# A fused attention and feed-forward kernel: another order of the output copies, another engine for the late ReLUs, and a rearranged end

## The chip, the cores and the metric

The kernel runs on one core of a Trainium2 chip. The metric is device time in microseconds (us) of one execution; lower is better. A core has TensorE (PE in the profile; its weight loads are the row PEld), VectorE (DVE), ScalarE (ACT), GpSimd (POOL) and SyncE (SP). The last one computes nothing and issues DMAs here. Every engine works through its own instructions in order and waits on semaphores for the others.

## The reference

Attention over 8 batches of 8 heads, 576 tokens and 64 columns a head, in which each row keeps only its 32 largest scores, and then a feed-forward layer:

```python
scores = scale * np.matmul(q, k.transpose(0, 1, 3, 2))
kth = np.partition(scores, -32, axis=-1)[..., -32:-31]
scores = np.where(scores >= kth, scores, -1e9)
attn = softmax(scores)                       # over the last axis
x = (attn @ v), heads side by side           # 4608 tokens x 512
h = x @ w_in                                 # 4608 x 2048
g = np.maximum(h, 0.0) + alpha * np.minimum(h, 0.0)
out = g @ w_out                              # 4608 x 512, float32
```

The kernel uses g = (1 - alpha) relu(h) + alpha h. It folds (1 - alpha) into `w_out`, and takes alpha h through a product `w_lin` of the two weight matrices, made once near the start. The output needs ReLU(h) alone, then, plus one small matmul from x.

## The kernel before, in words

All work is in `fast_path` (line 60). `Ordered` (line 17) wraps each engine, so that an engine's instructions run in the order in which the Python code issues them; every instruction's profile line is therefore L32, and groups are told apart by tile names. Only waits between engines are left to the framework. So what follows the code's order is each engine's queue; where two engines meet is a semaphore.

The unit of attention work is a **duo** (line 65): 128 query rows of each of two heads, against 576 keys. There are ND = 144 duos; a pair of heads makes several duos, and four pairs make a batch. The main loop (line 729) has one **slot** n for each duo, and in slot n each engine does a stage of another duo:

- PE: scores of duo n+1 (`st_qk`, tile `ps_sc`, three banks of PSUM with one buffer), weighted values of an older duo (`st_av`, tile `xo`), then feed-forward matmuls: `h_pe` makes one unit of h (16 or 8 matmuls into `ph`), `o_pe` a quarter of one output tile of 128 rows (five matmuls into `pz`). `keep_warm` fills gaps with matmuls on the tile `idle`, which holds zeros.
- ACT: two Sign passes that count entries above a trial threshold (`st_count`, tile `sg`), Exp of a masked duo into `w` (`st_exp`, line 400), at times the copy of a finished output tile from PSUM (`o_act`, line 579, tile `o_sb`), two ReLU passes that make the mask (`st_relu`, tile `r`), and the copy of the next scores out of PSUM (`st_exit`, tile `s_sb`).
- DVE: twelve MAX8 passes over the new scores, the threshold from them (`threshold_steps`; its last step, `turn`, writes `p`, which the Signs of the next slot need), the exact choice (`pick_steps`, tile `KZ`), the division by the softmax sum (`norm_a`, `norm_b`, tile `x`), and ReLU of h (`h_relu`, line 565, tile `gT`).
- POOL: two products a duo that feed the exact choice (`y`), and two subtractions that apply the mask (`s_sb<-s_sb,r`).
- SP: loads, the DMA transposes of `w` into `wT` (`st_wT`, line 405; its pool `three` has three buffers, line 101) and of `x` into `xT` (`st_xT`, line 468), and the stores of outputs.

Around the change: in a slot ACT's order is Signs, Exp, output copy, ReLUs, score copy (lines 745 to 764). Some even slots are **late** (line 743): too many units of h stand in line, so `dve_slot` has PE make one more (line 357) and its ReLU is taken by DVE at once, but from slot 118 on by ACT at the end of the slot (line 780). `h_relu` works from a queue, so the code's order decides which unit a call takes.

After the loop comes the **drain** (lines 815 to 903), written out by hand: the last duos (D = 143) pass their stages; D - 2, D - 1 and D are masked on DVE (`st_mask`: two products `w<-s_sb,KZ,e_sb` each) and D - 3 by Exp as in the loop; all are transposed by SP's DMA, multiplied by v (`st_av`), divided (`normed`, which also issues the DMA transpose into `xT` when a batch row block is complete), and then through h and the output. In the drain the scores' three banks are reused as one tile `spare` (line 818): bank 0 for every second output tile, banks 1 and 2 for the `xo` of the last four duos. Between these stages stand feed-forward calls as filling. The last block of 128 tokens can start its h only when the last duo has been divided and transposed; its 64 matmuls into `ph` and 20 into the output tile end the work, followed by one copy and one store. At the very end all engines read a flag that tells whether a slow general path must run (it doesn't here).

Of the kernel before, what the change touches and what calls it, by code (L numbers as in the profile page):

```python
# [8 lines left out]
FP32 = mybir.dt.float32  # L9
BF16 = mybir.dt.bfloat16  # L10
# [49 lines left out]
def fast_path(tc, q, k, v, moe_w_in, moe_w_out, moe_alpha, out, flag):  # L60
# [32 lines left out]
    with ExitStack() as ctx:  # L93
# [7 lines left out]
        three = pool("three", 3)  # L101
        gp = pool("gp", 4)
        xp = pool("xp", 4)
        ps_s = pool("ps_s", 1, space=PSUM)
        ps_d = pool("ps_d", 1, space=PSUM)
        ps_x = pool("ps_x", 1, space=PSUM)
        ps_h = pool("ps_h", 2, space=PSUM)
        ps_z = pool("ps_z", 1, space=PSUM)

        qv = q.rearrange("b h s d -> (b h) s d")  # L110
        kv = k.rearrange("b h s d -> (b h) s d")
# [204 lines left out]
        def dve_slot(n, f_late):  # L316

            norm = norm_of(n)
            rows = duos_at("count", n)
            picks = [f for m in duos_at("pick", n) for f in pick_steps(m)]  # L320
            s = T["s", n]
            if n % 2 == 0:
                T["up", n // 2] = two.tile([128, 4, NG // 2, 8], FP32, name="up", tag="up")
            up = T["up", n // 2]
            for i in range(2):
                r = 2 * (n % 2) + i
                for g in range(NG):
                    o = 24 * r + 8 * (g // 2)
                    m = DVE.max(out=(lo if g % 2 else up)[:, r, g // 2, :],
                                in_=s[:, i, GW * g:GW * g + GW])  # L330
                    if g % 2:
                        sm(m, [], [(o, o + 8)])
                        if picks:
                            picks.pop(0)()
            turn = None
            if n % 2:
                fold, negate, least, turn = threshold_steps(n // 2)
                fold()
                if n < ND - 1:
                    h_relu()  # L340
                negate()
            else:
                h_relu()
            for d in rows:
                row(d, 0)
            if turn:
                least()
                turn()
            if norm:
                norm_a(norm)  # L350
            for d in rows:
                row(d, 1)
            if norm:
                norm_b(norm)
            if f_late:
                h_pe()
                if n < 118:
                    h_relu()

        stage = {}  # L360

# [23 lines left out]
        def st_y(n):  # L385
            y = two.tile([128, 2, S], FP32, name="y", tag="y")
            sg = T.pop(("sg", n))
            for i in range(2):
                POOL.tensor_tensor(y[:, i, :], T["s", n][:, i, :], sg[:, i, :], ALU.mult)
            T["y", n] = y  # L390
# [20 lines left out]
        def st_av(n):  # L411
            d = duos[n]
            wt = T.pop(("wt", n))
            if ("xo", n // 2) not in T:
                if n < ND - 4:
                    T["xo", n // 2] = ps_x.tile([128, 2, 2, 65], FP32, name="xo", tag="x")
                else:
                    c = 512 * (1 + n // 2 - ND // 2 + 2)
                    T["xo", n // 2] = T["spare"][:, c:c + 260].rearrange("p (a b c) -> p a b c", a=2, b=2)
            xo = T["xo", n // 2][:, n % 2, :, :]  # L420
            for i in range(2):
                if d[0] == "n":
                    p = d[1]
                    for c in range(5):
                        K = 128 if c < 4 else 64
                        PE.matmul(xo[:, i, :], wt[0:K, 5 * i + c, :], v1[p][0:K, c, i, :],
                                  start=(c == 0), stop=(c == 4))
                else:
                    p = d[1 + i]
                    for h in range(2):  # L430
                        for c in range(5):
                            K = 128 if c < 4 else 64
                            PE.matmul(xo[64 * i:64 * i + 64, h, :], wt[0:K, 5 * i + c, 64 * h:64 * h + 64],
                                      v1[p][0:K, c, h, :], start=(c == 0), stop=(c == 4))
# [60 lines left out]
        def mlp_ready(xt, rows):  # L495
            ntok = sum(r[1] for r in rows)
            e_n = 512 // ntok
            tails = len(rows) > 1
            ch = {"done": 0}
            pieces = []  # L500
            for r0, m in rows:
                for o in range(0, m, 128):
                    pieces.append((r0 + o, min(128, m - o)))

            def unit(i):
                if i == 0:
                    ch["g"] = gp.tile([128, NFT, ntok], BF16, name="gT", tag="gT")
                ph = ps_h.tile([128, e_n, ntok], FP32, name="ph", tag="h")
                for e in range(e_n):
                    f = e_n * i + e  # L510
                    for kk in range(4):
                        if tails:
                            PE.matmul(ph[:, e, :].rearrange("p (b q) -> p b q", b=2),
                                      w_in_b[kk][:, 128 * f:128 * f + 128], xt[:, :, kk, :],
                                      start=(kk == 0), stop=(kk == 3))
                        else:
                            PE.matmul(ph[:, e, :], w_in_b[kk][:, 128 * f:128 * f + 128], xt[:, kk, :],
                                      start=(kk == 0), stop=(kk == 3))
                act.append((ch, e_n * i, e_n, ph))
            for i in range(NFT // e_n):  # L520
                soon.append((now[0] + (3 if now[0] < 116 else 2 if now[0] < ND else 0), lambda i=i: unit(i)))

            def part(t0, a):
                gt = ch["g"]
                if a == 0:
                    turns[0] += now[0] >= ND
                    if turns[0] % 2:
                        ch["z"] = T["spare"][:, 0:DMODEL]
                    else:
                        ch["z"] = ps_z.tile([128, DMODEL], FP32, name="pz", tag="z")  # L530
                z = ch["z"]
                if tails:
                    for b in range(2):
                        PE.matmul(z[64 * b:64 * b + 64, :], xt[:, b, a, :], w_lin_b[a], start=(a == 0), stop=False)
                else:
                    PE.matmul(z, xt[:, a, t0:t0 + 128], w_lin_b[a], start=(a == 0), stop=False)
                for f in range(4 * a, 4 * a + 4):
                    PE.matmul(z, gt[:, f, t0:t0 + 128], w_out_b[f // 4][:, f % 4, :],
                              start=False, stop=(f == NFT - 1))
                if a == 3:  # L540
                    stores.append((z, t0, pieces, now[0] + (now[0] < ND)))
            for t0 in range(0, ntok, 128):
                for a in range(4):
                    oq.append((ch, 4 * a + 4, lambda t0=t0, a=a: part(t0, a)))
# [34 lines left out]
        def o_act():  # L579

            if stores and stores[0][3] <= now[0]:
                z, t0, pieces, _ = stores.pop(0)
                o = io.tile([128, DMODEL], FP32, name="o_sb", tag="io")
                ACT.copy(o, z)
                at, left = 0, []
                for r0, m in pieces:
                    if t0 <= at < t0 + 128:
                        left.append((r0, at - t0, m))
                    at += m
                outs.append((o, left))  # L590
# [134 lines left out]
        for n in range(ND):  # L725
# [19 lines left out]
            for m in duos_at("count", n):  # L745
                st_count(m)
                st_y(m)
            for m in duos_at("exp", n):
                st_exp(m)
            if not norm_of(n):  # L750
                run(n, "ld")
            run(n, "lin_out")
            if ready() > 4 or not wide_copy:
                o_act()
            did = o_pe()
            run(n, "w")

# [18 lines left out]
                sm(DVE.tensor_copy(alpha_ps, aps), [], [(304, 320)])  # L776
                ACT.activation(alpha1m, aps, AF.Copy, scale=-1.0, bias=1.0)
            run(n, "scale")
            if late and n >= 118:
                h_relu(ACT)  # L780
            if norm_of(n):
                st_xT(norm_of(n) - 1)
                st_xT(norm_of(n))
# [10 lines left out]
        def st_mask(d):  # L794
# [5 lines left out]
            for i in range(2):  # L800
                DVE.scalar_tensor_tensor(out=w[:, i, 0:S], in0=s_[:, i, :], scalar=kt[:, i:i + 1],
                                         in1=e[:, i, :], op0=ALU.is_ge, op1=ALU.mult)
            st_wT(d)

        def normed(d):
            norm_a(d)
# [7 lines left out]
                    keep_warm()  # L814

        D = ND - 1
        now[0] = ND
        T["spare"] = ps_s.tile([128, 1536], FP32, name="spare", tag="s")
        o_sp()
        st_av(D - 6)  # L820
        h_pe(2)
# [46 lines left out]
        for _ in range(2):  # L868
            h_pe(2)
            h_relu(ACT)  # L870
        st_av(D - 2)
        h_pe(2)
        h_relu(ACT)
        st_av(D - 3)
        normed(D - 2)
        st_av(D - 1)
        h_pe(2)
        h_relu(ACT)
        st_av(D)
        normed(D)  # L880
        now[0] += 2
        o_pe()
# [301 lines left out]
```

## Time and profile before

| what | us |
|---|---|
| median of 3 runs (815.65 to 817.17) | 816.7 |
| the profiled execution's own time | 816.19 |
| its span, first to last instruction | 814.4 |
| PE, DVE, ACT, POOL busy | 734.9, 750.8, 770.4, 748.1 |
| mean granted clock of TensorE (1 is full) | 0.988 |

The profile comes from one execution. Its span leaves 1.79 us of the execution's time outside. A row of a timeline gives start, duration, engine, line, operation, the tiles written and read, shapes and count; a bracket at its end is the idle time before it and what ended it. A row of the chain of waits gives start, duration and the work that the end of the program waited for. A row of a table by stretches gives, for each engine, busy time and in brackets instructions, then the granted clock and the DMA engines' share.

### The profile page before, as it was taken

Reading aid. Unit: us, or ns where it says so; the run is one execution under the profiler, and the core shown is the slowest. Engines: PE = TensorE matmul, PEld = TensorE weight load, DVE = VectorE, ACT = ScalarE, POOL = GpSimd, SP = SyncE. Lnnn points to the kernel's source line nnn. Section 1 sums busy time; section 2 is a strip of 40 time slices with the busy share of each in tenths; the row PEclk is TensorE's granted clock in tenths of the full one; section 3 lists DMA queues with packets and bytes.
Section 4 is the critical chain, followed back from the end, with each engine's and each line's share of the span. In section 5 each row is a group of like instructions: output and inputs, shape, how many; then the busy total and the mean of one; then the engine's idle time right before and its main releaser. Section 6 shows DMA issues by size and latency. Waiting matters only on the chain.

```text
span 814.4 us, 17835 instructions
## 1 busy us (share of the span) xinstructions
PE 734.9 (90%) x5362; PEld 423.5 (52%) x5434; DVE 750.8 (92%) x3459; ACT 770.4 (95%) x1270; POOL 748.1 (92%) x704
## 2 busy tenths in 40 slices
PE   8888899989889998989889998998989999899986
PEld 5334455555545554555545554555545555455663
DVE  4999999999999999999999999999999998999841
ACT  5999999999999999999999999999999999999951
POOL 2999999999999999999999999999999998999930
PEclk9999999999999999999999999999999999999989
DMA  7699996556656565566656565555665664544461
GB/s 158 174 191 185 161 165 115 102 122 125 136 112 132 111 129 118 116 119 134 128 114 128 111 126 122 127 120 107 142 123 122 114 119 100 93 96 75 98 114 37
DMA packets 343497, 100.25 MB, mean 123 GB/s; under 512 B 337424, under 2 KB 337440, under 8 KB 343392
## 3 DMA queue, kind: packets, MB, share of 16 engines
q1 hardware_dynamic: 340240, 91.63, 57.1%
q0 software_dynamic: 1952, 7.09, 3.6%
q8 instruction: 45, 0.74, 0.4%
q14 instruction: 60, 0.49, 0.2%
q10 hardware_dynamic: 1200, 0.30, 0.2%
HBM read 36.71 MB, written 9.44 MB: 57 GB/s over the span
## 4 chain that ended last, share of the span: by engine, by line
DVE 29%; ACT 28%; PE 20%; POOL 10%; issue 8%; DMA 3%; SPq 0%; ACTq 0%; POOLq 0%; DVEq 0%
DVE small L32 9%; ACT r L32 8%; ACT sg L32 7%; DVE p L32 7%; ACT s_sb L32 6%; DVE up L32 6%; PE pz L32 5%; POOL s_sb L32 5%; PE ps_sc L32 5%; ACT w L32 4%; POOL y L32 4%; PE ph L32 4%; DVE gT L32 3%; PE xo L32 2%; DMA wT<-w 2%
## 5 line engine op out<-in xcount | busy, mean ns | idle before, releaser
L32 POOL TENSOR_TENSOR y<-s_sb,sg 128x576 f32<-128x576 f32 x288 | 362.1, 1278 | 23.4 <-ACT sg L32 23.3
L32 POOL TENSOR_TENSOR s_sb<-s_sb,r 128x576 f32<-128x576 f32 x282 | 355.1, 1280 | 9.1 <-ACT r L32 8.7
L32 DVE MAX8 up<-s_sb 128x8 f32<-128x96 f32 x864 | 212.1, 245 | 15.3 <-ACT s_sb L32 15.0
L32 ACT ACTIVATE sg<-s_sb,p 128x576 bf16<-128x576 f32 x288 | 221.4, 774 | 2.8 <-DVE p L32 1.4
L32 DVE MAX8 p<-y 128x8 f32<-128x576 f32 x288 | 215.3, 748 | 7.9 <-POOL y L32 7.3
L32 DVE MAX8 small<-s_sb 128x8 f32<-128x96 f32 x864 | 216.2, 250 | 0.0
L32 ACT ACTIVATE r<-s_sb,KZ 128x576 bf16<-128x576 f32 x282 | 202.6, 769 | 0.3 <-DVE KZ L32 0.3
L32 PE MATMUL ps_sc<-qkT 64*128 64x512 f32 (+2 forms) x768 | 185.0, 572 | 14.7 <-ACT s_sb L32 14.6
L32 ACT ACTIVATE w<-s_sb 128x1152 bf16<-128x1152 f32 x141 | 163.1, 1157 | 1.7 <-POOL s_sb L32 0.9
L32 ACT COPY s_sb<-ps_sc 128x1152 f32<-128x1152 f32 x144 | 159.1, 1105 | 4.1 <-PE ps_sc L32 4.0
L32 PE MATMUL ph<-xT,w_in_b 128*128 128x256 bf16 (+1 forms) x1472 | 150.3, 250 | 5.6 <-ACT qkT L32 3.7
L32 PEld LDWEIGHTS <-w_in_b 128*128 128x128 bf16 x1472 | 120.4, 98 | 47.3 <-issue 10.1
L32 PE MATMUL pz<-w_out_b,gT 128*128 128x512 bf16 x515 | 134.2, 379 | 9.7 <-issue 6.2
L32 PE MATMUL xo<-v,wT 128*128 128x65 bf16 (+1 forms) x1560 | 123.5, 198 | 0.6 <-DMA wT<-w 0.4
L32 PEld LDWEIGHTS <-wT 128*128 128x128 bf16 (+3 forms) x1600 | 98.0, 100 | 33.2 <-DMA wT<-w 3.9
L32 PEld LDWEIGHTS <-gT 128*128 128x128 bf16 x576 | 54.5, 98 | 74.0 <-issue 18.7
L32 PEld LDWEIGHTS ps_sc<-kd,qkT 128*128 128x128 f32 x256 | 38.5, 189 | 98.4 <-issue 98.4
L32 DVE TENSOR_SCALAR gT<-ph 128x512 bf16<-128x512 f32 x126 | 84.8, 673 | 4.8 <-PE ph L32 4.8
L32 PEld LDWEIGHTS ps_sc<-qkT 64*128 64x128 f32 (+1 forms) x768 | 55.7, 170 | 57.9 <-issue 29.2
L32 PE MATMUL ps_sc<-kd,qkT 128*128 128x128 f32 x256 | 63.1, 329 | 0.0
L32 PE MATMUL rest<-idle 128*128 128x512 bf16 x196 | 50.0, 380 | 6.8 <-DVE gT L32 4.7
L32 ACT ACTIVATION_READ_ACCUMULATOR sg<-s_sb,p 128x1 f32 x288 | 56.1, 195 | 0.0
(68 smaller groups left out, 584.2 us busy)
## 6 DMA issues: line engine op xcount, KB each, us to landing
k_st<-in_k_dram SPq DMA_DIRECT2D x64, 128.0 KB, 2.9
v_st<-in_v_dram SPq DMA_DIRECT2D x64, 128.0 KB, 2.8
q_st<-in_q_dram SPq DMA_DIRECT2D x62, 128.0 KB, 2.7
out_dram<-o_sb SPq DMA_DIRECT2D x30, 256.0 KB, 2.5
w_st<-in_moe_w_out_dram POOLq DMA_DIRECT2D x4, 1024.0 KB, 6.5
wT<-w SPq DMA_TRANSPOSE x144, 3.5
w_in_b<-in_moe_w_in_dram POOLq DMA_DIRECT2D x4, 512.0 KB, 6.0
k_st<-in_k_dram SPq DMA_DIRECT2D x32, 32.0 KB, 3.0
```

Source lines behind the costliest of these rows:

```text
L32: ins = self.tc.keep_in_program_order(f(*a, **kw))
```

## The change

It has five parts.

1. In the main loop `o_act()` is called before `st_exp` in place of after it.
2. In late slots from 118 on, ReLU of the extra unit is DVE's, as in earlier slots.
3. In the drain the pool of the scores is closed, and a new pool takes its three banks as three tiles: two `xo2`, one `pz2`. There is no `spare`.
4. The last duo's weights are not transposed by DMA. `turn_w` has PE transpose them in ten steps against an identity, into two PSUM tiles in the banks of `xo` and `pz`; `turned` copies one of these by DVE, one by ACT into a `wT` tile. POOL writes the identity into `idle` at the start of the drain. With it `st_av(D)` moves ahead of `st_av(D - 3)`, and one unit of h moves between `turn_w` and `turned`.
5. The last output tile is copied in halves, columns 256 to 511 by DVE and 0 to 255 by ACT, and stored in halves by SP's and ACT's queues.

```diff
-        ps_s = pool("ps_s", 1, space=PSUM)
...
+        scores = ctx.enter_context(ExitStack())
+        ps_s = scores.enter_context(tc.tile_pool(name="ps_s", bufs=1, space=PSUM))
...
                 h_pe()
-                if n < 118:
-                    h_relu()
+                h_relu()
...
-                    c = 512 * (1 + n // 2 - ND // 2 + 2)
-                    T["xo", n // 2] = T["spare"][:, c:c + 260].rearrange("p (a b c) -> p a b c", a=2, b=2)
+                    T["xo", n // 2] = ps_e.tile([128, 2, 2, 65], FP32, name="xo2", tag=f"x{n // 2 % 2}")
...
-                        ch["z"] = T["spare"][:, 0:DMODEL]
+                        ch["z"] = ps_e.tile([128, DMODEL], FP32, name="pz2", tag="z2")
...
                 o = io.tile([128, DMODEL], FP32, name="o_sb", tag="io")
+                if now[0] > ND and not (soon or hq or act or oq or stores):
+                    DVE.tensor_copy(o[:, 256:512], z[:, 256:512])
+                    ACT.copy(o[:, 0:256], z[:, 0:256])
+                    r0 = pieces[0][0]
+                    ACT.dma_start(out[r0:r0 + 128, 0:256], o[:, 0:256])
+                    SP.dma_start(out[r0:r0 + 128, 256:512], o[:, 256:512])
+                    return
                 ACT.copy(o, z)
...
+            if ready() > 4 or not wide_copy:
+                o_act()
             for m in duos_at("exp", n):
                 st_exp(m)
...
-            if ready() > 4 or not wide_copy:
-                o_act()
             did = o_pe()
...
-            if late and n >= 118:
-                h_relu(ACT)
...
-            st_wT(d)
+            if d < D:
+                st_wT(d)
+
+        def turn_w(d):
+            ps = [p.tile([128, 5, 128], BF16, name="wTp", tag=t) for p, t in ((ps_x, "x"), (ps_z, "z"))]
+            for i in range(2):
+                for c in range(5):
+                    PE.transpose(ps[i][:, c, :], ws[d % 4][:, i, 128 * c:128 * c + 128], idle)
+            return ps
+
+        def turned(d, ps):
+            wt = T["wt", d] = three.tile([128, 10, 128], BF16, name="wT", tag="wT")
+            DVE.tensor_copy(wt[:, 0:5, :], ps[0])
+            ACT.copy(wt[:, 5:10, :], ps[1])
...
         D = ND - 1
+        POOL.tensor_copy(idle, ident_f)
         now[0] = ND
-        T["spare"] = ps_s.tile([128, 1536], FP32, name="spare", tag="s")
+        scores.close()
+        ps_e = pool("ps_e", 1, space=PSUM)
...
         for _ in range(2):
             h_pe(2)
             h_relu(ACT)
+        ps = turn_w(D)
+        h_pe(2)
+        turned(D, ps)
+        h_relu(ACT)
         st_av(D - 2)
+        st_av(D)
         h_pe(2)
         h_relu(ACT)
         st_av(D - 3)
         normed(D - 2)
         st_av(D - 1)
-        h_pe(2)
-        h_relu(ACT)
-        st_av(D)
         normed(D)
```

## The prediction

> **What bounds the kernel now.** I read the page first, then a table by stretches, the waits of each engine in the loop, and the chain of waits and the timelines of the end. The table gives, for each stretch, busy time of PE, PEld, DVE, ACT and POOL, the granted clock, and the DMA share:
>
> ```profile
> 120.00:620.00 500.00, 455.20 (x3297) 263.40 (x3345) 491.83 (x2289) 496.73 (x811) 493.78 (x448) 1.00 0.59 121
> 620.00:770.00 150.00, 141.69 (x1162) 85.32 (x1176) 140.57 (x656) 146.94 (x244) 141.98 (x125) 1.00 0.53 103
> 770.00:814.40 44.40, 32.74 (x320) 22.13 (x324) 15.19 (x33) 17.36 (x30) 11.19 (x12) 0.89 0.36 75
> ```
>
> From 120 to 620 three engines are at 98 to 99%: ACT can't gain from another order of its own instructions, only from less work, and only as far as DVE and POOL follow. From 620 to 770 ACT stays at 98% and DVE falls to 94%. In the last 44.4 us nothing is full: a chain decides there. Its pieces (start, duration, work):
>
> ```profile
> 782.25 5.73 DMA wT<-w
> ...
> 788.02 1.08 PE spare L32 x10
> ...
> 789.20 0.19 DVE KZ L32
> ...
> 789.41 0.43 DVE x L32
> ...
> 789.89 1.04 PE spare L32 x10
> 790.93 1.82 PE ph L32 x16
> 792.75 0.89 PE spare L32 x10
> ...
> 793.97 3.28 PE pz L32 x14
> 797.25 1.79 PE ph L32 x32
> ...
> 806.94 0.59 ACT o_sb L32
> ```
>
> A DMA transpose, that of duo D-3, ends at 787.98. Then come the matmuls of D-3, the division of its pair on DVE, the matmuls of D-1, a unit of h, and the matmuls of D. Only then can the last row block be divided, transposed and sent through h. These timeline rows carry the terms below:
>
> ```profile
> 780.59 3.11 DVE L32 SCALAR_TENSOR_TENSOR w<-s_sb,KZ,e_sb 128x576 bf16<-128x576 f32 x4
> ...
> 782.00 1.96 PE L32 MATMUL ph<-xT,w_in_b 128*128 128x128 bf16 x32
> ...
> 785.77 0.79 PE L32 MATMUL spare<-v,wT 128*128 128x65 bf16 x10 [1.81 <-DMA wT<-w]
> ...
> 786.59 1.93 SPq L32 DMA_TRANSPOSE wT<-w  x1
> ...
> 789.89 1.04 PE L32 MATMUL spare<-v,wT 128*128 128x65 bf16 x10 [0.80 <-DVE x L32]
> ...
> 794.34 1.19 SPq L32 DMA_TRANSPOSE xT<-x  x1
> ...
> DMA to landing us min/median/max: 2.4/2.9/3.4
> ```
>
> The last one is the landing of the two transposes into `xT`; the later one, in a quiet queue, is taken at 2.4.
>
> **The end, step by step.** I redo the chain on the old clock.
>
> *Start.* POOL's write of `idle` is a cast of 128x128; the nearest rows are 0.29 and 0.40 us (below). It stands ahead of the four `y` products in a queue without idle time, so 0 to 0.3 us reach DVE's choice. DVE next waits for PE anyway, so I take 0.1. Two units of h then run from 782.1 to 784.05, and the masked weights of D are ready at 783.7 (780.59 + 3.11).
>
> *Transposes on PE.* Ten weight loads with matmuls of 128 columns; 32 of that size take 1.96 us, 0.061 each, so 0.6 us, to 784.7. They lie in PE's idle time ahead of 785.77. The unit of h moved behind them (16 x 0.061) ends at 785.65, again in that idle time.
>
> *The new wait.* `st_av(D - 2)` runs at 785.8 to 786.65, as its DMA allows. `turned` needs a `wT` buffer, and of three the free one is that of D-2. The trace shows that wait already: SP issued the fourth transpose at 786.59, when `st_av(D - 2)` ended (785.77 + 0.79 = 786.56). So both copies start at about 786.7. Behind ACT's stands one ReLU, and PE's `st_av(D)` waits for both. Their lengths come from rows of the same engines:
>
> ```profile
> L32 DVE COPY qkT<-tps 128x512 f32<-128x512 f32 x31 | 21.0, 678 | 4.8 <-PE tps L32 4.8
> L32 DVE COPY qkT<-tps 128x128 f32<-128x128 f32 x26 | 7.3, 280 | 0.4 <-PE tps L32 0.4
> L32 ACT COPY s_sb<-ps_sc 128x1152 f32<-128x1152 f32 x144 | 159.1, 1105 | 4.1 <-PE ps_sc L32 4.0
> L32 ACT COPY o_sb<-pz 128x512 f32<-128x512 f32 x34 | 19.3, 569 | 6.8 <-PE pz L32 6.8
> L32 ACT COPY qkT<-tps 128x128 f32<-128x128 f32 x6 | 1.6, 271 | 0.0
> L32 POOL CAST v<-v_st 128x256 bf16<-128x256 f32 x64 | 25.3, 399 | 0.0
> L32 POOL CAST v<-v_st 64x128 bf16<-64x128 f32 x32 | 9.3, 289 | 0.0
> ```
>
> DVE's 640 elements extend the first two rows to 0.8 us (0.68 if 16-bit input were quicker), ACT's lie between 569 and 1105 ns, about 0.7. `st_av(D)` then goes from 787.55 to 788.35.
>
> *Rest.* The fourth unit of h ends at 789.3. `st_av(D - 3)`, whose weights are there since 787.98, ends at 790.1. `st_av(D - 1)` writes a bank of its own; the 0.80 us wait for DVE's `x` shows that inside one tile it had to wait although it wrote other columns. It ends at 790.9. Division (0.19 + 0.43 and two handovers) gives the `xT` transpose at 791.6 in place of 794.34, landing at 794.0. Meanwhile PE does three quarters of the output tile before. They took 3.6 us (from 793.64 to 797.25) with a slow start, and I take 3.4: to 794.3. So what is late next is PE again, with the DMA 0.3 us ahead of it. From there the order is the old one. **Gain 2.9 us**, from 794.3 against 797.25.
>
> **The clock.** Part of this hangs on TensorE's clock:
>
> ```profile
> 783.90:787.30 3.40, 1.58 (x26) 1.35 (x26) 0.00 (x0) 0.60 (x1) 0.00 (x0) 1.00 1.17 191
> 787.30:790.70 3.40, 2.24 (x25) 1.44 (x22) 0.61 (x2) 0.60 (x1) 0.00 (x0) 0.50 0.88 162
> ...
> 548.40:551.80 3.40, 2.11 (x15) 1.35 (x16) 3.40 (x11) 3.40 (x7) 3.40 (x4) 1.00 0.51 96
> 551.80:555.20 3.40, 2.85 (x22) 1.62 (x21) 3.37 (x20) 3.40 (x6) 3.40 (x4) 1.00 0.22 46
> ```
>
> After a stretch with PE busy 46% of the time (1.58 of 3.40, one gap of 1.81 us) the clock was 0.50, and the h unit at 790.93 took 1.82 us where the row at 782.00 gives 0.98. After one with 62% (2.11 of 3.40) it stayed 1.00. In the new order the only gaps there are 0.15 and 0.9 us, 70% busy, so I take full speed throughout. The Trainium skill (TensorE: Matmul & The Clock Gate, section Why this matters for your kernels) warns of idle gaps above about 3 us; the gap here was 1.81 us, and the clock fell all the same, so the trace differs. By that page's rule the clock could not fall in the new order and the sum would stand; by the rows a little more idle time would do it, a rival below.
>
> **The last output.** One copy of 569 to 590 ns becomes two of 256 columns, each about halfway between 271 and 569 on ACT, 280 and 678 on DVE: 0.4. Side by side the end comes 0.2 us sooner, one after the other 0.25 us later; halved stores may land somewhat sooner or, on a second queue, not. I take +0.1, between -0.3 and +0.3. The Trainium skill (PSUM — Partial Sum Buffer, section PSUM bank collisions raise a hardware error) says that reads of one bank by ScalarE and VectorE at once collide and have to be kept apart; no row of before shows such a pair. By it the copies would stand in series, and the term would be +0.25.
>
> **The loop.** Rows from the waits of PE (120 to 770 us), of ACT and DVE (629 to 766 or 769; total, times, longest), the late ReLUs on ACT, DVE's ReLU, and one late slot:
>
> ```profile
> PE pz L32 <- ACT o_sb L32: 15.0, 17, 1.5
> ...
> ACT gT L32 <- PE ph L32: 2.3, 3, 0.9
> L32 ACT ACTIVATE gT<-ph 128x512 bf16<-128x512 f32 x7 | 4.2, 599 | 2.4 <-PE ph L32 2.3
> DVE up L32 <- ACT s_sb L32: 6.4, 11, 0.8
> L32 DVE TENSOR_SCALAR gT<-ph 128x512 bf16<-128x512 f32 x126 | 84.8, 673 | 4.8 <-PE ph L32 4.8
> ...
> 645.60 0.26 DVE L32 MAX8 up<-s_sb 128x8 f32<-128x96 f32 x1
> 646.49 0.60 ACT L32 ACTIVATE gT<-ph 128x512 bf16<-128x512 f32 x1 [0.92 <-PE ph L32]
> 650.41 0.17 DVE L32 TENSOR_SCALAR p<-small 128x4 f32<-128x4 f32 x1
> 651.88 0.78 ACT L32 ACTIVATE sg<-s_sb,p 128x576 bf16<-128x576 f32 x1
> ```
>
> *Output copies earlier.* The same instructions on ACT: Exp starts 0.57 us later 30-odd times, and its transpose is used two slots (10 us) later. By its due time in the code (line 541) the tile copied was finished in an earlier slot. PE gets its bank about 1.1 us sooner (Exp's length), which removes most of 15.0 us of PE's waits. But ACT's score copies wait for PE only 4.0 us in the whole execution (their row above), so PE's time is hidden nearly everywhere. I take -0.1, between -4.0 (all those waits gone) and +1.0 (a copy here and there that now waits for PE).
>
> *Late ReLUs.* ACT loses seven (4.2 us) and their waits (2.3): 6.5 us. DVE gains seven of 0.67, 4.7 us, and it must wait for PE's unit too, since it comes to it earlier. In the slot shown DVE would start the ReLU at 646.49 and its next MAX8 at 647.1, not at 645.60: 1.5 late. Its threshold `p` comes at 652.1, not at 650.6, and the Signs that need it, at 651.88 before, start at 652.1. ACT was freed 1.5 us earlier and spends that waiting. So the gain on ACT is not the loop's. The loss isn't either: DVE idles 6.4 us waiting for `s_sb` in that stretch, and these waits take up the delay between late slots. I take -0.2, between -6.5 (ACT alone bounds) and +7.0 (4.7 + 2.3, nothing absorbed).
>
> **Sum.** -2.9 - 0.1 - 0.2 + 0.1 = -3.1 us, on a span of 814.4: 811.3. The profiled execution took 816.19, so 813.1; the median of the runs is 0.5 higher, and would give 813.6. I say **813.3**. A measurement of this kernel can tell about 0.2%, 1.6 us, from no change.
>
> **Rivals.**
> - *ACT was the bound from 629 to 769.* For it: ACT at 98%, DVE at 94%. Against: the slot above. All 6.5 us would give 807, half 810.2. Chance 0.09.
> - *DVE becomes the bound there: slower.* Each late ReLU delays `p`, ACT's Signs wait, and so does all else. Price up to 7.0 us, so 813.5 + 7.0 = 820.5. It decides once DVE's waits absorb less than 4 of these 7.0 us. For it: 93.7% busy before 4.7 us are added to 150. Against: 6.4 us of waits, spread between these slots. Chance 0.10.
> - *The clock halves in the drain all the same.* An h unit costs 0.85 more and each of two or three `st_av` 0.25: 1.5 us, 814.8. Chance 0.12.
> - *The new wait eats the drain.* The copies of the transposed weights come later than 787.5, or the framework still ties the banks together; the chain then ends on PE some 0.8 us earlier only: 815.5. Chance 0.09.
>
> **How the numbers follow.** The forecast, 812 to 814.8, has 0.60. Below 815.1, faster by over 0.2%: forecast, first rival, and half of the third, 0.76. Within 0.2%: the rest of the third and the fourth, 0.14. Slower: 0.10. The range leaves out most of the first rival and the slower case: 810.6 to 816.2.
>
> **What would show it.** Right: no DMA for the last `wT`, the last `xT` transpose 9.5 us after the drain's h pair starts (now 794.34 - 782.00 = 12.3), clock 1.00 up to the end, DVE's waits for `s_sb` in the late stretch shrunk, and Signs there beginning just behind `p`, with the loop's end unmoved. Wrong: PE waiting over 1 us ahead of `st_av(D)`, a clock of 0.50 near 790, ACT waiting for `pz` in the loop, or the loop's last slots moved by over 1 us.

## The result and the profile after

| what | before | after |
|---|---|---|
| median of 11 runs each (lowest to highest), us | 817.02 (815.65 to 820.12) | 812.79 (811.65 to 815.55) |
| ratio of after to before, 95% interval | | 0.9952 (0.9935 to 0.9969) |
| the profiled execution's own time, us | 816.19 | 815.49 |
| its span, us | 814.4 | 813.1 |
| mean granted clock of that execution | 0.988 | 0.987 |

The forecast was 813.3. The profiled execution of after is one of its longer ones: of its 11 runs four took 814.85 to 815.55 at a mean clock of 0.987, the others 811.65 to 813.56 at 0.990 to 0.998. So this trace is not that of the median, and the difference turns out to be the main point.

The table by stretches of after (columns as in the prediction: PE, PEld, DVE, ACT, POOL, clock, DMA):

```profile
120.00:620.00 500.00, 456.55 (x3296) 262.45 (x3345) 491.60 (x2288) 496.43 (x811) 494.07 (x447) 1.00 0.59 121
620.00:770.00 150.00, 143.29 (x1170) 85.68 (x1185) 144.22 (x666) 144.49 (x237) 142.59 (x127) 1.00 0.53 104
770.00:813.10 43.10, 34.00 (x329) 22.26 (x331) 15.73 (x34) 17.37 (x30) 11.08 (x12) 0.87 0.34 68
```

From 620 to 770 ACT has lost 2.45 us of work and DVE has gained 3.65; both stand at 96% now. In the last stretch the clock is no better than before (0.87 beside 0.89).

The chain of waits of after, at the end:

```profile
780.61 5.15 DMA wT<-w
...
785.80 0.81 PE xo L32 x10
...
786.63 0.50 DVE wT L32
...
787.18 0.79 PE xo L32 x10
787.97 1.44 PE ph L32 x16
789.41 1.89 PE xo L32 x20
...
792.06 4.52 PE pz L32 x13
796.58 1.79 PE ph L32 x32
```

It is the chain that was forecast: the DMA transpose of an older duo, the product of D - 2, the copy of PE's transposes into a buffer that this product sets free, the product of D. But each piece of PE from 787.97 on is slow: 1.44 us for a unit of h, 4.52 for 13 matmuls into `pz` that were put at 3.4. The clock tells why; the rows lie on the clock's own steps of 3.4 us:

```profile
784.90:788.40 3.50, 2.12 (x31) 1.58 (x30) 0.49 (x1) 1.19 (x2) 0.00 (x0) 0.99 0.86 225
788.40:791.80 3.40, 3.40 (x32) 2.47 (x31) 1.04 (x4) 0.60 (x1) 0.00 (x0) 0.50 0.00 0
791.80:795.20 3.40, 3.18 (x9) 1.22 (x8) 0.18 (x1) 0.00 (x0) 0.00 (x0) 0.50 0.19 39
795.20:798.60 3.40, 3.40 (x41) 2.47 (x39) 1.09 (x2) 0.00 (x0) 0.00 (x0) 1.00 0.02 5
```

After a stretch in which PE was busy 2.12 of 3.50 us (61%), 6.8 us ran at half clock, as long as in before.

To see where time comes from, I cut each trace at four events: the score copies on ACT of slots 10, 118 and 143 (the loop's last), the end of the last matmul, the end of the span. Durations in us:

```
                      slot 10   10 to 118   118 to 143   143 to last   last matmul   half clock
                      begins    (loop)      (late loop)  matmul        to end        in the drain
before                59.49     568.55      136.52       42.30         7.55          6.8
after                 59.72     568.46      136.04       41.96         6.91          6.8
e1_loop_only          59.27     568.55      136.04       43.70         6.31          10.2
e2_drain_only         59.69     568.74      136.53       41.81         7.50          6.8
e3_no_halves          61.50     568.54      136.07       39.13         6.33          none
e4_banks_only         59.75     568.70      136.53       42.06         7.61          6.8
e5_fill               59.71     568.32      135.98       39.16         7.08          none
e8_own_first_whole    61.49     568.31      135.95       38.13         6.28          none
e9_before_fill        59.70     568.49      136.51       42.06         7.59          3.4
e10_sp_31             59.71     568.31      136.01       41.85         8.69          6.8
p1_copy_only          59.12     568.50      136.08       42.37         6.27          6.8
p2_late_only          59.12     568.74      136.57       43.78         7.57          10.2
```

How far can the columns be trusted? e2, e4 and e9 have before's loop, and took 568.49 to 568.74 us from slot 10 to 118 and 136.51 to 136.53 from 118 to 143; the six kernels with after's loop took 135.95 to 136.07 there. So the first of these two columns tells nothing below some 0.2 us, the second some 0.1.

In the profiled pair the loop gives -0.57 (-0.09, which is within that spread, and -0.48, which is not), the drain only -0.34, the tail behind the last matmul -0.64; the loop was reached 0.23 later, and the part outside the span grew from 1.79 to 2.39. Three things in this were not in the forecast: a drain that gains next to nothing in this execution, a tail that gets shorter though the last output costs more, and an outside part that grows.

### The profile page after: what moved, and what is told of

It reads as the page before. It is cut to its first block, busy times and chain, and to the rows that moved or that the text cites. A ratio compares the mean times of both kernels' runs of the same rounds, so it can differ in the third digit from the quotient of the medians.

```text
span 813.1 us, 17839 instructions
## 1 busy us (share of the span) xinstructions
PE 739.2 (91%) x5375; PEld 423.2 (52%) x5448; DVE 754.6 (93%) x3468; ACT 767.4 (94%) x1264; POOL 748.6 (92%) x705
## 4 chain that ended last, share of the span: by engine, by line
DVE 36%; ACT 21%; PE 16%; POOL 15%; issue 7%; DMA 3%; SPq 1%; ACTq 0%; POOLq 0%; DVEq 0%
DVE small L32 12%; DVE p L32 8%; POOL y L32 7%; POOL s_sb L32 7%; DVE up L32 7%; ACT sg L32 5%; ACT r L32 5%; ACT s_sb L32 5%; PE pz L32 5%; DVE gT L32 4%; PE ps_sc L32 4%; ACT w L32 4%; PE ph L32 4%; PE xo L32 2%; DMA wT<-w 2%
## 5 line engine op out<-in xcount | busy, mean ns | idle before, releaser
L32 PE MATMUL pz<-w_out_b,gT 128*128 128x512 bf16 x545 | 143.5, 382 | 9.5 <-issue 5.9
L32 PE MATMUL xo<-v,wT 128*128 128x65 bf16 (+3 forms) x1600 | 127.2, 199 | 3.0 <-DMA wT<-w 1.7
L32 DVE TENSOR_SCALAR gT<-ph 128x512 bf16<-128x512 f32 x133 | 89.7, 674 | 9.3 <-PE ph L32 9.3
L32 PE MATMUL rest<-idle 128*128 128x512 bf16 x200 | 52.4, 389 | 6.9 <-DVE gT L32 4.8
```

Source lines behind the costliest of these rows:

```text
L32: ins = self.tc.keep_in_program_order(f(*a, **kw))
```

## The experiments

Theory: the gain is the drain's, and depends on the clock staying full there; the loop gives a few tenths. Rivals: the gain is the loop's, or it sits in the tail. Medians of these kernels mix executions of different clock (and two profiled executions, e3's and e8's, reached slot 10 some 1.8 us late), so terms are read from the stretches above, and medians say what came out in all.

### The loop alone, the drain alone, the whole last copy, the banks

e1_loop_only is before with parts 1 and 2:

```diff
-                if n < 118:
-                    h_relu()
+                h_relu()
...
+            if ready() > 4 or not wide_copy:
+                o_act()
             for m in duos_at("exp", n):
...
-            if ready() > 4 or not wide_copy:
-                o_act()
...
-            if late and n >= 118:
-                h_relu(ACT)
```

> The two edits of the loop alone (output copies ahead of Exp, late ReLUs on DVE), the drain as before. My theory: the gain is the drain's, so this is within 0.5 us of before, ratio 0.9994 to 1.0; in the trace the late stretch (slots 118 to 143) is 0 to 0.6 us shorter, Signs of even slots start 0.03 us behind the threshold p, and DVE waits less for s_sb. Rival (the loop gives the gain, ACT being the bound from 629 us on): 3 to 4 us faster than before, ratio 0.9955.

Measured: 815.17 us, ratio 0.9972 (0.996 to 0.9985). The loop gives 0.48 us and the tail 1.24; its drain, at half clock for 10.2 us, is longer than that of before. So the loop's two edits bring 2.45 us to the median, and most of it outside the loop. That is more than my theory gave (0.5 at most) and less than the rival (3 to 4): neither had the tail.

e2_drain_only is after with parts 1, 2 and 5 undone, e3_no_halves with part 5 alone undone; shown is part 5:

```diff
-                if now[0] > ND and not (soon or hq or act or oq or stores):
-                    DVE.tensor_copy(o[:, 256:512], z[:, 256:512])
-                    ACT.copy(o[:, 0:256], z[:, 0:256])
...
-                    return
```

> The drain's edits alone (three banks, PE transposes, new order), the loop as before and the last output as one copy and one store. My theory: 3 to 4 us faster than before, ratio 0.9955, with the xT transpose of the last block 2.3 us sooner after the drain's first unit of h where the clock halves and 2.8 where it doesn't. Rival (loop): under 0.5 us faster.

> The changed kernel with its last output in one copy on ACT and one store on SP. Theory: the halves were copied one after the other (DVE 0.43, ACT 0.37 us), so one copy of 0.59 us ends 0.25 us sooner and this is 0.1 to 0.3 us faster than the changed kernel. Rival (halved stores land sooner by more than that): 0.1 to 0.4 us slower than the changed kernel. Both are near what the runs can tell, so the trace's time from the last matmul to the landing decides.

Measured: e2 813.44 us, ratio 0.9959 (0.9944 to 0.9974); e3 813.65, ratio 0.9952 (0.9935 to 0.9969). e2's profiled drain ran at half clock and took 41.81 us, 0.5 less than before; five of its seven runs, at 813.08 to 813.59 and a clock of 0.989 to 0.995, were some 2.5 us shorter than that profiled one (816.04); a run of 815.4 had a clock of 0.995, so not every longer run is the clock's. The last `xT` transpose of e2's trace comes 1.8 us sooner after the drain's h pair than in before (10.6 beside 12.3), not the 2.3 expected at half clock. e3's profiled drain kept the full clock and took 39.13, 3.2 less than before, and there it comes 2.9 us sooner (9.4), as expected. The tail of e3 is 0.58 shorter than that of after: the halves cost, they don't bring. (The medians don't tell it: both ratios are 0.9952.) The timeline of after and its stores (the last number is the us from issue to landing) show how:

```profile
806.28 0.43 DVE L32 COPY o_sb<-pz 128x256 f32<-128x256 f32 x1 [4.57 <-PE pz L32]
806.73 0.34 SPq L32 DMA_DIRECT2D out_dram<-o_sb  x1
806.74 0.37 ACT L32 COPY o_sb<-pz 128x256 f32<-128x256 f32 x1 [3.16 <-DVE o_sb L32]
807.14 0.38 ACTq L32 DMA_DIRECT2D out_dram<-o_sb  x1
```

```profile
out_dram<-o_sb SPq DMA_DIRECT2D x1, 128.0 KB, 1.7
out_dram<-o_sb ACTq DMA_DIRECT2D x1, 128.0 KB, 4.2
```

ACT's half starts when DVE's ends, with a wait for it in its row: one after the other, 0.83 us in place of 0.59, as the Trainium skill (PSUM — Partial Sum Buffer, section PSUM bank collisions raise a hardware error) would have it. SP's half then lands after 1.7 us, but ACT's after 4.2, at 811.4; e3's whole 256 KB landed 2.9 us after their issue.

e4_banks_only is before with part 3 alone:

```diff
-                        ch["z"] = T["spare"][:, 0:DMODEL]
+                        ch["z"] = ps_e.tile([128, DMODEL], FP32, name="pz2", tag="z2")
...
-        T["spare"] = ps_s.tile([128, 1536], FP32, name="spare", tag="s")
+        scores.close()
+        ps_e = pool("ps_e", 1, space=PSUM)
```

> The three banks as three tiles alone; transposes by DMA, the old order, the old loop. Theory: the 0.64 us for which st_av(D - 1) waited for DVE's x goes, and nothing else: the last xT transpose starts 0.4 to 0.7 us sooner, 816.4 against 817.0, ratio 0.9993. Rival (the wait was the bank's or the pair's and not the tile's): the wait stays, ratio 1.

Measured: 816.48 us, ratio 0.9992 (0.9981 to 1.0002), which doesn't tell it from no change. In the trace the 0.80 us wait for DVE's `x` is gone (0.14 us are left ahead of that product) and the last `xT` transpose comes 0.4 us sooner, as expected; the drain is 0.24 shorter, at half clock for 6.8 us.

### The clock: the same drain with PE's gaps filled

e5_fill is after with seven matmuls on the tile `idle` in PE's two gaps; nothing reads their result:

```diff
+        def top_up(k):
+            t = ps_e.tile([128, DMODEL], FP32, name="rest2", tag="z2")
+            for _ in range(k):
+                PE.matmul(t, idle, idle.unsqueeze(1).to_broadcast([128, 4, 128]), start=True, stop=True)
...
         ps = turn_w(D)
         h_pe(2)
+        top_up(4)
         turned(D, ps)
         h_relu(ACT)
         st_av(D - 2)
+        top_up(3)
         st_av(D)
```

> The changed kernel with PE's two gaps in the drain filled by seven matmuls into an unused bank (four ahead of st_av(D - 2), three ahead of st_av(D)). Theory (the spread of the runs, and most of the drain's gain, is the granted clock: TensorE is halved for 6.8 us after the gaps in some executions and not in others): no 0.50 stretch between 780 and 805, all runs near the fast group of the changed kernel, 811.5 to 813, median 812.0, mean clock 0.99 or more. Rival (the groups come from something else): median as the changed kernel, 812.8, with runs at 815 as before.

Measured: 812.72 us, ratio 0.9939 (0.9922 to 0.9956), all six runs between 812.16 and 812.96. The rows of e5 on the clock's steps:

```profile
785.20:788.60 3.40, 3.38 (x41) 2.10 (x39) 0.49 (x1) 1.19 (x2) 0.00 (x0) 1.00 0.88 231
788.60:792.00 3.40, 3.40 (x34) 2.06 (x32) 1.22 (x4) 0.60 (x1) 0.00 (x0) 1.00 0.00 0
```

Nothing but idle time was filled, and the clock stays full: the drain takes 39.16 us in place of 41.96. That is the price of the halving in the new order, 2.8 us; e3, whose clock stayed full without filling, took 39.13. The median is that of after, since most runs of after seem to have kept their clock anyway; what the filling takes away is the spread, 0.8 us in place of 3.9 (of six runs, none of which can have started 1.8 us late beside the others). SP pauses for 1.0 us at the end of this kernel too, but this is a plain wait: ACT's half of the output lands at 808.52, 4.4 us after its issue, and the event that waits for its semaphore follows at 808.54.

e9_before_fill puts eight such matmuls into the 1.81 us gap of before:

```diff
+        t = ps_z.tile([128, DMODEL], FP32, name="rest2", tag="z")
+        for _ in range(8):
+            PE.matmul(t, idle, idle.unsqueeze(1).to_broadcast([128, 4, 128]), start=True, stop=True)
         st_av(D - 2)
```

> The kernel before with nothing changed but eight matmuls into an unused bank in PE's gap of 1.81 us in the drain. Clock theory: the clock stays at 1.00 there, the two h units and the later matmuls go at full speed, and the median falls from 817.6 to 815, to where the two fastest runs of before lie (814.7 and 815.0, mean clock 0.996). Rival (drain's length is the order's and the DMA's, not the clock's): 817 to 817.6.

Measured: 815.96 us, ratio 0.998 (0.9969 to 0.9992). About 1 us, not the whole price; the table by stretches of e9 shows why:

```profile
784.20:787.60 3.40, 3.10 (x30) 1.80 (x29) 0.00 (x0) 0.60 (x1) 0.00 (x0) 1.00 1.28 179
787.60:791.00 3.40, 2.21 (x34) 1.68 (x31) 0.61 (x2) 0.60 (x1) 0.00 (x0) 1.00 0.94 172
791.00:794.40 3.40, 3.40 (x28) 2.26 (x26) 0.61 (x2) 0.60 (x1) 0.00 (x0) 0.50 0.00 0
```

The first stretch, filled to 91%, is no longer followed by half clock, but the next, with the waits for the DMA and for DVE's `x` still in it (65%), is: one step of 3.4 us in place of two.

How busy is busy enough? In the twelve traces, a stretch of 39 to 62% in the drain was followed by half clock each time (before, after, e1, e4, e10, p1, p2), one of 91% or more never (e5, e8, e9). In between it goes either way: 67% in e2 was followed by it, and 64% in e3 was not:

```profile
785.00:788.50 3.50, 2.35 (x36) 1.77 (x33) 0.49 (x1) 1.25 (x3) 0.00 (x0) 0.99 0.82 174
788.50:791.90 3.40, 3.40 (x35) 2.86 (x36) 0.48 (x2) 0.60 (x1) 0.00 (x0) 0.50 0.26 56
```

```profile
785.60:789.00 3.40, 2.16 (x35) 1.73 (x32) 0.41 (x1) 0.96 (x2) 0.00 (x0) 1.00 1.29 186
789.00:792.40 3.40, 3.26 (x47) 2.62 (x48) 0.78 (x4) 1.38 (x3) 0.00 (x0) 1.00 0.32 73
```

(e2 above, e3 below.) The loop has both as well. In after's trace the steps at 600.60 and 655.20 us, with PE busy 1.90 and 1.97 of 3.40 us (56 and 58%), were not followed by half clock. Over all steps of the twelve traces from 6 us to the last matmul, counted by the records of which some can be missing: of those at full clock, all 23 with PE busy 45% or less were followed by half clock, 14 of 130 between 46 and 67%, and none above. What decides in between stays open: the busy share alone does not. That the steps lie differently against the program in each execution, and so cut the same gaps in one or in two, fits the spread of after's runs, but is argued.

### The tail: SP's instructions

In before, SP pauses for 1.33 us among its last instructions, between two semaphore events at 811.55 and 812.88. It does so in e2, e4, e9 and p2 too (1.24 to 1.36), but not in after, e1, e3, e8 and p1, nor in e5 but for the wait told above. The first group executes 882 to 884 instructions on SP, the second 853 to 855: with the output copies ahead of Exp, SP has 29 or 30 waits fewer to make. e10_sp_31 is after with 31 instructions on SP that do nothing:

```diff
         normed(D)
+        for _ in range(31):
+            SP.drain()
```

> The changed kernel with 31 empty instructions (drains) on SP in the drain, where SP is idle. Theory: the changed kernel's SP program has 30 waits fewer than before's, and with that a pause of 1.3 us among SP's last instructions, seen in before, disappeared; with 31 added the pause is back, the time from the last matmul to the end is 8.2 us in place of 6.9, and the time rises by 1.3 us. Rival (the pause has another cause): 6.9 us, no change.

Measured: 815.36 us, ratio 0.9962 (0.9944 to 0.9979), and the tail is 8.69 us, 1.78 more than after's and 0.5 more than expected; the pause is 1.60 us. The median is 2.6 above after's, twice what was expected, but mixes clocks: half of the runs show 0.986. The rows list what SP executes for the line with which the program ends; the two times are the first and the last start. Before, then p1 (told below), then e10:

```profile
L1179 SPq EVENT_SEMAPHORE  x14: 17/28/28, 811.4 to 814.3; - x14
L1179 SPq DRAIN  x3: 7/7/13, 813.5 to 813.8; - x3
```

```profile
L1179 SPq EVENT_SEMAPHORE  x14: 17/28/28, 810.7 to 812.3; - x14
L1179 SPq DRAIN  x3: 7/7/13, 811.5 to 811.8; - x3
```

```profile
L1202 SPq EVENT_SEMAPHORE  x14: 17/28/28, 811.4 to 814.5; - x14
L1202 SPq DRAIN  x3: 7/7/13, 813.7 to 814.0; - x3
```

From its first event to its first drain SP needs 2.1 us in before, 0.8 in p1 and 2.3 in e10. So the pause goes and comes with the number of SP's instructions: shown. Its place says the same. Counted in the traces, it stands ahead of the 870th instruction that SP executes in before, e2, e4, e9 and p2, though in e2 another wait is the 870th, and ahead of the 869th in e10. That it is a fetch of instructions is argued: the Trainium skill (Runtime: NRT & Kernel Launch, section Instruction fetch mechanics) says that instructions are fetched in blocks and that a taken branch breaks the prefetch, and SP has just passed the branch on the flag. No run here shows the fetch itself: a transfer of instructions (8 KB) is on its way when before's pause begins (811.36 to 811.80), but after has one at 811.36 to 811.77 and no pause, and the records don't tell for which engine.

With the halves, part of what is saved comes back outside the span: that part is 2.55 us in the median of after's runs and 2.57 in e5's, but 1.78 in e10's, which has the pause, as in before's. Without the halves it doesn't follow the pause: 1.82 in p1 and 1.99 to 2.07 in e1, e3 and e8, which have none, 1.79 in e2 and e4, 1.82 in e9 and 1.96 in p2, which have it.

### Part 1 and part 2 apart

p1_copy_only is before with the output copies ahead of Exp, p2_late_only with the late ReLUs on DVE:

```diff
+            if ready() > 4 or not wide_copy:
+                o_act()
             for m in duos_at("exp", n):
...
-            if ready() > 4 or not wide_copy:
-                o_act()
```

```diff
-                if n < 118:
-                    h_relu()
+                h_relu()
...
-            if late and n >= 118:
-                h_relu(ACT)
```

> Before with part 1 alone: the output copies stand ahead of Exp. Theory: these copies give two things. Score copies of slots 100 to 118 come 0.13 us sooner (94.30 to 94.17 us) and those of slots 118 to 143 about as much (136.5 to 136.4); and SP loses some 30 waits, so that it executes about 854 instructions in place of 884 and the pause of 1.3 us among its last ones goes: last matmul to end 6.3 in place of 7.5 us. Sum -1.5 us, 815.5 beside 817.0. Rival: the pause goes by the late ReLUs, and the copies give only the loop's 0.1 to 0.2: 816.8, last matmul to end 7.5.

> Before with part 2 alone: the late ReLUs from slot 118 on taken by DVE. Theory: slots 100 to 118 as before (94.30 us), slots 118 to 143 shorter by 0.3 to 0.5 (136.52 to about 136.1), SP's 884 instructions and the pause of 1.3 us at the end stay (last matmul to end 7.5): -0.4 us, 816.6 beside 817.0. Rival, that the ReLUs bring nothing by themselves and all of the loop's gain is the copies': 136.5, 817.0.

Measured: p1 814.28 us, ratio 0.9962 (0.9949 to 0.9974); p2 817.21, ratio 1.000 (0.999 to 1.0009). The copies give all of the loop's gain, -0.49 from slot 10 to slot 143 and most of it in the late stretch (136.08), and SP's 1.28 us of tail; p2 gives nothing, its late stretch is 136.57. I had expected the late stretch the other way round, and so the rival of p2's expectation is right. p1's profiled execution (814.13) agrees with this: -0.37 ahead of slot 10, -0.49, +0.07 in the drain and -1.28 are -2.07, and it is 2.06 below 816.19. Its median is 3.1 below that of before: its runs spread from 812.0 to 816.3, and I read the rest as the clock, which no trace shows.

How do earlier copies help a loop in which ACT is full? The waits of PE from 120 to 770 us, in before 15.0 us for `o_sb`, are in p1 and in p2:

```profile
PE ps_sc L32 <- ACT s_sb L32: 13.6, 28, 1.0
```

```profile
PE pz L32 <- ACT o_sb L32: 14.3, 16, 1.5
...
PE ps_sc L32 <- ACT s_sb L32: 4.2, 11, 0.8
```

In p1 PE no longer waits for a bank, and waits 8.9 us longer for ACT to read the scores instead (4.7 us in before). It is earlier with what stands between, the units of h, and for a few of these ACT waits. One late ReLU in p1, then the same one in before:

```profile
743.14 0.60 ACT L32 ACTIVATE gT<-ph 128x512 bf16<-128x512 f32 x1 [0.43 <-PE ph L32]
```

```profile
743.98 0.60 ACT L32 ACTIVATE gT<-ph 128x512 bf16<-128x512 f32 x1 [0.77 <-PE ph L32]
```

0.34 us shorter, and the interval between the score copies of this slot and the one before is 0.34 shorter as well. Shorter are also slot 118 (by 0.16) and slots 133 to 135 (by 0.24), and slot 120 is 0.14 longer; these I did not follow further.

Why do DVE's ReLUs give nothing? The waits of ACT and then DVE from 629 to 766 us in p2:

```profile
ACT sg L32 <- DVE p L32: 4.2, 6, 1.7
...
DVE gT L32 <- PE ph L32: 3.4, 6, 1.0
DVE up L32 <- ACT s_sb L32: 1.1, 3, 0.4
```

ACT had no wait for `p` among these in before; the late ReLUs have turned its 6.5 us into waits of 4.2 us for DVE and shorter ones for others. DVE waits 1.1 us for scores in place of 6.4. A late slot now ends up to 1.51 us sooner, and the next one is longer by 1.79.

### The wait that the change adds, taken away

e8_own_first_whole is e3 with a free buffer for the transposed weights and the product of D ahead of that of D - 2:

```diff
-            wt = T["wt", d] = three.tile([128, 10, 128], BF16, name="wT", tag="wT")
+            wt = T["wt", d] = two.tile([128, 10, 128], BF16, name="wTd", tag="y")
...
-        st_av(D - 2)
         st_av(D)
+        st_av(D - 2)
```

> The changed kernel with a buffer of its own for the last transposed weights (a free one of y), so that the copies needn't wait for st_av(D - 2); st_av(D) goes ahead of st_av(D - 2) into PE's gap; the last output in one copy and one store. Theory: the wait of 0.58 us ahead of st_av(D) and the gap of 0.80 ahead of st_av(D - 2) both go, the clock stays up, the last xT transpose starts 26.2 us after the last score copy (26.86 without the halving, 27.79 with it), and the median is 811.3, 1.5 us under the changed kernel. Rival (DMA landing of the other duos sets the end, so nothing is won): as the kernel without halves at full clock, 26.9 and 812.

Measured: 810.49 us, ratio 0.9914 (0.9896 to 0.9932), the lowest median here, 2.3 us below after's and 0.8 below the 811.3 expected. Its timeline:

```profile
785.42 0.49 DVE L32 COPY wTd<-wTp 128x640 bf16<-128x640 bf16 x1 [0.43 <-PE wTp L32]
785.70 0.69 ACT L32 COPY wTd<-wTp 128x640 bf16<-128x640 bf16 x1
...
786.39 0.78 PE L32 MATMUL xo<-v,wTd 128*128 128x65 bf16 x10
787.30 0.79 PE L32 MATMUL xo<-v,wT 128*128 128x65 bf16 x10
```

The copies no longer wait for a product, and the product of D fills the time in which PE had waited for the DMA of D - 2. The drain takes 38.13 us at full clock, 1.0 less than in e3.

## Why the prediction was right, point by point

The time was right to 0.5 us. The chain forecast for the drain is the one that ran, and where the clock stayed full it had the forecast's length. That the sum came out is in part luck: the clock stayed full in most executions only, not for the reason given, and the terms around the drain were off and cancel.

**The drain (-2.9).** At full clock it is -3.2 (39.13 and 39.16 in place of 42.30). The rows of after, beside the steps:

```profile
781.60 1.95 PE L32 MATMUL ph<-xT,w_in_b 128*128 128x128 bf16 x32
...
783.39 0.72 PE L32 MATMUL wTp<-idle,w 128*128 128x128 bf16 x10
...
783.95 1.06 PE L32 MATMUL ph<-xT,w_in_b 128*128 128x128 bf16 x16
785.80 0.79 PE L32 MATMUL xo<-v,wT 128*128 128x65 bf16 x10 [0.80 <-DMA wT<-w]
786.63 0.69 ACT L32 COPY wT<-wTp 128x640 bf16<-128x640 bf16 x1 [2.44 <-PE xo L32]
786.63 0.49 DVE L32 COPY wT<-wTp 128x640 bf16<-128x640 bf16 x1 [3.17 <-PE xo L32]
787.18 0.79 PE L32 MATMUL xo<-v,wT 128*128 128x65 bf16 x10 [0.58 <-DVE wT L32]
...
792.00 1.19 SPq L32 DMA_TRANSPOSE xT<-x  x1
```

The transposes took 0.72 us (forecast 0.6), and the copies began at 786.63 for the reason given, the buffer of D - 2 (5.03 us after the h pair's start, forecast 4.7). ACT's copy took 0.69 (0.7), DVE's 0.49 (0.8; even the bound for 16-bit input was 0.68). PE waited 0.58 us ahead of the product of D, under the 1 us that would have spoken against the forecast. The last `xT` transpose is issued 10.4 us after the h pair's start at 781.60 (9.5 forecast, 12.3 before), at half clock; at full clock it is issued after 9.4 us in e3 and 9.5 in e5.

**"So I take full speed throughout": the step that failed.** I foresaw gaps of 0.15 and 0.9 us and a stretch 70% busy. Counted from the start of the h pair, PE was through with the unit behind its transposes after 3.41 us (forecast 3.65), and the weights of D - 2 let it go on after 4.20 (forecast 3.8): a wait of 0.80 in place of 0.15. With the 0.58 behind it the stretch was 61% busy, and the clock halved in the profiled execution: 0.50 near 790, one of the forecast's own signs of being wrong. The rival with the halved clock (0.12, 1.5 us) came true in 4 of 11 runs, if their clock of 0.987 means what it means in the traced one. Their median lies 3.0 us above that of the other seven, near the price of 2.8. The mean clock alone doesn't prove it: p1's traced execution had 0.992 with 6.8 us of half clock in the drain, since its clock fell for one step of 3.4 us ahead of 90 us and after's for three. Its price was 2.8, not 1.5: the halved 6.8 us hold 13 matmuls into `pz` too, which the price left out. The forecast's row of 62% followed by full clock is no threshold either. The section of the Trainium skill that the prediction named (TensorE: Matmul & The Clock Gate, section Why this matters for your kernels) warns of gaps above about 3 us only; here gaps of 0.80 and 0.58 us were enough, and by the measurement its rule is no safeguard.

How much of the -3.2 is a shorter chain and how much the clock? At half clock in both the drain gains 0.3 to 0.5 (after, e2). Beside e1 to e4, two of the 26 runs of before came to 814.71 and 814.96 at a clock of 0.996, and its median was 817.62. If these two kept the full clock in the drain, then e2's runs at 813.1 to 813.6 are the same with the shorter chain, which is worth some 1.5 us by that, and the clock the other half. No trace of such a run of before exists, so this split is argued. e9 bounds it: the old order with 3.4 us at half clock took 42.06, and these 3.4 us can have cost 1.7 at most, since PE does half its work in them. So at full clock the old order takes an estimated 40.4 to 42.1 us, and the shorter chain is worth 1.2 to 2.9 (against 39.16). The forecast's 2.9 mixed the two: it set the new order at full clock against an old one whose 6.8 us at half clock it took as they stood.

**The loop (-0.1 and -0.2).** The sum was about -0.5 in place of -0.3 (-0.57 in the profiled pair, with the spread told above), and the two terms were wrong both ways: the copies gave all of it, about -0.5 (p1), the late ReLUs nothing (p2). The reasoning for the late ReLUs held to the row: `p` was forecast at 652.1, with the Signs behind it:

```profile
652.07 0.17 DVE L32 TENSOR_SCALAR p<-small 128x4 f32<-128x4 f32 x1
652.27 0.78 ACT L32 ACTIVATE sg<-s_sb,p 128x576 bf16<-128x576 f32 x1 [1.69 <-DVE p L32]
```

The gain on ACT went into waiting for DVE, and DVE's own waits took up the delay. Both rivals of the loop (ACT the bound, 807 to 810; DVE the bound, 820.5) fall with p2's 1.000. For the copies I looked at ACT's waits for scores alone, and missed its waits for a unit of h, 2.3 us, which stood in the prediction's own rows.

**The last output (+0.1).** The upper bound of its range, +0.25 in series, is what the copies did; the later landing on ACT's queue makes it +0.58 in the span, and outside the span another 0.56 (2.55 beside 1.99 in e3).

**Not in the forecast: SP's tail, -1.28.** The end of the program was taken as fixed. Tail and outside part together are 9.33 us in before (7.55 and 1.78) and 9.46 in after (6.91 and 2.55): the pause that went pays for the halves, and the +0.13 that is left stands by luck beside the forecast's +0.1.

**The sum again.** From 816.19: slot 10 0.23 later, loop -0.57, drain -3.14 at full clock, SP's pause -1.28, halves +0.64 by the tail (6.91 beside p1's 6.27), outside the span +0.77 (2.55 beside 1.78): 812.84; the median is 812.79. With -0.34 for the drain and the traced 2.39 outside it is 815.47, beside the traced 815.49; this second sum must close, since the stretches fill the time. (The forecast's chances, added up from its rivals, are 0.75 below 815.1 and 0.15 within 0.2%, where it has 0.76 and 0.14.)

## What to carry to other kernels

At a hand-made end, count TensorE's idle time over stretches of some 3.4 us and not gap by gap: gaps of 0.6 and 0.8 us that each look harmless cost 2.8 us together in the traced execution, and matmuls that nobody reads, or better another order of real work, keep the clock. Work taken from a full engine is worth nothing if it goes to the engine that the first one waits for next; ask for the chain through both. Compare also the tail behind the last result, where a change in how many waits an engine makes can move more than a change in the work.

## What the hardware showed that I had not expected

- TensorE's granted clock moves in steps of 3.41 us, and in the drain steps with PE 39 to 62% busy were each followed by 6.8 to 10.2 us at 0.50; in after's loop steps of 56 and 58% were not.
- SP paused 1.2 to 1.6 us near its end with 882 to 884 instructions executed (before, e2, e4, e9, p2, e10), and not there with 853 to 855; the pause stood ahead of the 870th (in e10 the 869th).
- DVE copied 640 16-bit elements from PSUM in 0.49 us, where 512 of 32 bits take 0.68; ACT took 0.69 for the same 640.
- A store of 128 KB on ACT's queue landed 4.2 us after its issue, one of the same size on SP's queue, 0.4 us earlier, after 1.7.
